# Paired FFN products on 64 rows beside the attention scores

## The chip, the core and the metric

The kernel runs on one core of a Trainium2 chip. The core has a matrix engine (TensorE, PE in the profile, with its weight loads as PEld), a vector engine (VectorE, DVE), a scalar engine (ScalarE, ACT), GpSimd (POOL) and SyncE (SP); each works through its own queue in order, and the queues wait for each other by semaphores. In this kernel POOL and SP mostly issue DMAs. The metric is the device time of one execution in microseconds (us), lower is better. Before the change it is 320.61 us, the median of 6 runs (319.83 to 321.36).

## What is computed

Attention with a bias by distance for 8 batches of 8 heads, 576 positions and 64 elements a head; the heads' outputs side by side are the input of a feed-forward network (FFN) with a maximum of three products:

```python
scores = q @ k.T / sqrt(64) + bias            # per batch and head, 576 x 576
attn = exp(scores - max) / sum(exp(...))
x = (attn @ v)                                # -> 4608 tokens x 512
h = maximum(maximum(x @ w1, x @ w2), x @ w3)  # 512 -> 768
out = h @ w_out                               # 768 -> 512
```

## The kernel before

**Attention by head pairs.** Two heads of 64 elements share the 128 partitions: head `par` of a pair lies on rows 64*par to 64*par+63 of the transposed queries and keys `qT` and `kT`. The main loop (line 813) goes over batches 1 to 7 and the four head pairs of each; (b, hp) names one, from 0. The 576 positions are four tiles of 128 and a left-over of 64.

- `visit` (line 554) makes the scores of 256 queries, c = 0 or 1, against the four key tiles: two groups of four matmuls, each on 64 rows, the two heads at once in two banks, and one exponential over each group into the tile `e4`. With `el` given it makes the scores of the 64 left queries (`scq`) first, in two banks of `ps_a`.
- `left_keys` makes the scores of the 64 left keys of both heads (`sct`) in one product on 128 rows.
- The bias enters as a product of exponentials: `times_band`, `times_bandt` and `times_band_left` multiply a band of `e4` or `el` on VectorE.
- `attend` (line 604; its matmuls are on line 94 in the profile, tile `a`) multiplies the exponentials by the values for half of the queries: 18 matmuls in half 0, 27 in half 1. The `quotients` that it returns divide on VectorE (a reciprocal, then a multiplication into `x_sb`). A head pair's two halves run in the next head pair, from the list `late`: half 0 after the first visit, half 1 in the hook `keys`.

**FFN between them.** A batch's tokens are turned by DMA transposes into `xT`. `ffn` makes, for a chunk of 512 tokens, six blocks of 128 hidden columns: `first` (a product of four matmuls over 128 rows each and 512 columns; copied by ScalarE into `m0`), `second` (product; VectorE's maximum with `m0` gives `m`) and `third` (product; maximum with `m` gives a block of `hT`), and then four `output` products of six matmuls each, copied to `osb` and stored through SP. These pieces wait in the list `pending` with their number of matmuls; `fill(target)` (line 439) takes pieces up to that number and puts hooks between them. In most head pairs there are two fills of up to 13, one before and one after the second visit, so a head pair holds 24 FFN matmuls.

**What holds the order.** Instructions passed to `inorder` keep the program's order on their engine; all matmuls do. PSUM (the matmuls' output memory) has eight banks: `ps_s` has two tiles of two banks for scores, `ps_a` two of one bank for `attend` (and `scq`, and some products), `ps_f` two of one bank for FFN products. A tile's next user waits until the last reader of the one before is done. `go_behind` makes given instructions wait for another one. `idle_sums` marks fills in which `first` may take a `ps_a` bank. On SP's queue stand, in program order, the stores of outputs (`store_outputs`), the DMA transposes of the next batch's q and k (`crossbar`, ten a batch, two at a time) and those of `x_sb`.

Of the kernel before, what the change touches and what calls it, by code (L numbers as in the profile page):

```python
# [10 lines left out]
F32 = mybir.dt.float32  # L11
# [28 lines left out]
def kernel(  # L40
# [52 lines left out]
    def mm(*args, **kw):  # L93
        inorder(nc.tensor.matmul(*args, **kw))  # L94
# [11 lines left out]
    def act_copy(out_, in_):  # L106
        return inorder(nc.scalar.activation(out=out_, in_=in_, func=ACTF.Copy))  # L107
# [206 lines left out]

    def ffn(t0, nt, last):
        hT = ffnw.tile([P, FCH * CH], BF16, tag="hT", name="hT")
        per = CH // nt
        n_fb = FCH // per  # L320
        st = [{} for _ in range(n_fb)]

        def product(ps, fb, ki):
            for i in range(per):
                cf = fb * per + i
                for c in range(DCH):
                    mm(
                        ps[:, i * nt : i * nt + nt], lhsT=w_bf[ki][:, c, cf * P : cf * P + P],
                        rhs=xT[:, c, t0 : t0 + nt], start=(c == 0), stop=(c == DCH - 1),
                    )  # L330

        def bank(name):
            return ps_f.tile([P, CH], F32, tag="ff", name=name)

        def block(fb):
            return hT[:, fb * CH : fb * CH + CH]

        def first(fb):
            ps0 = ps_a.tile([P, CH], F32, tag="a", name="ps0") if last or idle_sums else bank("ps0")
            product(ps0, fb, 0)  # L340
            if per > 1:
                nc.scalar.activation(out=block(fb), in_=ps0, func=ACTF.Copy)
                return
            st[fb]["m0"] = ffnw.tile([P, CH], BF16, tag="m0", name="m0")
            nc.scalar.activation(out=st[fb]["m0"][:], in_=ps0, func=ACTF.Copy)  # L345

        def second(fb):
            ps1 = ps_s.tile([P, 2 * CH], F32, tag="sc", name="ps1")[:, 0:CH] if last else bank("ps1")
            product(ps1, fb, 1)
            if per > 1:  # L350
                inorder(nc.vector.tensor_tensor(out=block(fb), in0=ps1, in1=block(fb), op=ALU.max))
                return
            m = st[fb]["m"] = ffnw.tile([P, CH], BF16, tag="m", name="m")
            inorder(nc.vector.tensor_tensor(out=m[:], in0=ps1, in1=st[fb]["m0"][:], op=ALU.max))  # L354

        def third(fb):
            ps2 = bank("ps2")
            product(ps2, fb, 2)
            other = block(fb) if per > 1 else st[fb]["m"][:]
            inorder(nc.vector.tensor_tensor(out=block(fb), in0=ps2, in1=other, op=ALU.max))  # L360

        def output(j):
            osb = osbp.tile([P, d_model], F32, tag="osb", name="osb")
            r0 = t0 + j * P

            def columns(ps, c0, c1):
                for cf in range(FCH):
                    mm(
                        ps, lhsT=hT[:, cf * nt + j * P : cf * nt + j * P + P], rhs=wo_bf[:, cf, c0:c1],
                        start=(cf == 0), stop=(cf == FCH - 1),  # L370
                    )

            if r0 + P == NTOK:
                c = d_model - P
                for copy, c0, c1, pool, tag, eng in (
                    (dve_copy, 0, c, ps_f, "ff", nc.sync), (act_copy, c, d_model, ps_a, "a", nc.scalar)
                ):
# [12 lines left out]
            if last:  # L390
                store()
            else:
                stores.append(store)

        f, m, g = ([(DCH, lambda fn=fn, fb=fb: fn(fb)) for fb in range(n_fb)] for fn in (first, second, third))
        o = [(FCH, lambda j=j: output(j)) for j in range(nt // P)]
        if per == 1:
            portions = [[f[0], m[0]]]
            for fb in range(1, n_fb):
                portions.append([g[fb - 1], f[fb], m[fb]])  # L400
            portions.append([g[-1], (0, None), o[0]])
        else:
            if not t0:
                portions = [[f[0]], [m[0], f[1]], [m[1]], [f[2], m[2]]]
                deferred.append(([[g[0]], g[1:]], [[x] for x in o]))
                o = []
            else:
                portions = [x for gs, _ in deferred for x in gs]
                for fb in range(n_fb):
                    portions += [[f[fb], m[fb]], [g[fb]]]  # L410
                portions += [x for _, os in deferred for x in os] + [[o[0]]]
                o = o[1:]
        if len(o) > 2:
            portions.append(o[1:3])
        return portions, o[-1:]

    pending, rest, stores, deferred, idle_sums = [], [], [], [], []

    def store_outputs():

# [115 lines left out]
            ))  # L536

    def exp(out_, in_):
        nc.scalar.activation(out=out_, in_=in_, func=ACTF.Exp, scale=inv_sqrt_d)  # L539

    def put_left_queries(el, banks):

# [4 lines left out]
    def turn_left_queries(qT, kT, banks):  # L547

        for t in range(KT):
            for par, bank in enumerate(banks):  # L550
                r = slice(64 * par, 64 * par + 64)
                mm(bank[:, 64 * t : 64 * t + 64], lhsT=kT[r, P * t : P * t + P], rhs=qT[r, QM:S])

    def visit(qT, kT, e4, c, mid=None, el=None):

        if el is not None:
            banks = [ps_a.tile([P, KT * 64], F32, tag="a", name="scq") for _ in range(2)]
            turn_left_queries(qT, kT, banks)
            put_left_queries(el, banks)
        for tt in range(0, KT, 2):  # L560
            sc = ps_s.tile([P, 2, 2, QS], F32, tag="sc", name="sc")
            for t in range(2):
                for par in range(2):
                    r = slice(64 * par, 64 * par + 64)
                    mm(
                        sc[:, par, t, :], lhsT=kT[r, P * (tt + t) : P * (tt + t) + P],
                        rhs=qT[r, c * QS : c * QS + QS],
                    )
            exp(e4[:, tt : tt + 2, :, c * QS : c * QS + QS].rearrange("p t h q -> p h t q"), sc[:])
            if tt == 0 and mid:  # L570
                mid()

# [9 lines left out]


    def times_bandt(hp, el):
        inorder(nc.vector.tensor_tensor(
            out=el[:, S - 192 : S], in0=el[:, S - 192 : S], in1=bandt[:, hp, :], op=ALU.mult
        ))

    def left_queries(hp, qT, kT, el):

        sc = ps_s.tile([P, 2, CH], F32, tag="sc", name="scq")
        turn_left_queries(qT, kT, [sc[:, par, 0 : KT * 64] for par in range(2)])
        eq = el[:, S:].rearrange("p (t h q) -> p h t q", t=KT, h=2)
        exp(eq, sc[:, :, 0 : KT * 64].rearrange("p h (t q) -> p h t q", t=KT))

    def times_band_left(hp, el):
        last_tile = el[:, S + P * KT - P :].rearrange("p (h q) -> p h q", h=2)
# [160 lines left out]
    for hp in range(HP):  # L758
# [7 lines left out]
        def keys():  # L766
            left_keys(hp, qT, kT, el, QS, S)
# [45 lines left out]
    for b, hp in [(b, hp) for b in range(1, B) for hp in range(HP)]:  # L813
# [2 lines left out]
        qT, kT = (x[:, hp, :] for x in qk[b])  # L816
        e4, el = e_tiles()
        together = b > 1 and (b, hp) != (2, 0)
        rate = 8 if b == 1 or (b, hp) == (2, 0) else 13


# [12 lines left out]
        if turned:  # L834
            turned.pop(0)()
        quotients = next_late()
        times_band(hp, e4, 0, 0, QS, inorder)
        quotients()
        if b == 1 and hp + 1 < HP:
            spread_packed(hp + 1, nc.vector)  # L840
# [5 lines left out]
            if together:  # L846
                next_late()()

        fill(rate, keys, *([lambda: None] if together else []))
        times_bandt(hp, el)  # L850


        visit(qT, kT, e4, 1, el=el if together else None)
        store_outputs()
        if b == 1 or hp in (1, 2) and b + 1 < B:
            next(crossbar, None)
# [7 lines left out]
        if b == 1 and hp + 1 < HP:  # L864
            second_transposes(qk[1], hp + 1)
        if hp == 1 and b > 1:
            add_ffn((b - 1) * CH, CH)
        if hp == (2, 2, 0)[min(b, 3) - 1] and b + 1 < B:
            if b == 1:
                load_last_weights(turned_qk[2, 1, 1])  # L870
# [14 lines left out]
            for t in range(1 if together else 2, 3):  # L885
                times_band(hp, e4, t, 0, QM, inorder)

        if together:
            idle_sums.append(hp)
        fill(rate, bands_2, queries)  # L890
        idle_sums.clear()
        times_band_left(hp, el)
        for half in range(2):
            late.append(lambda b=b, hp=hp, e4=e4, el=el, half=half: attend(b, hp, e4, el, half))

    while late:
        store_outputs()
        early()
        next_late()()
        fill(13)  # L900
# [38 lines left out]
```

The softmax here doesn't subtract the row's maximum and nothing guards it: scores larger than these inputs give would overflow.

## Time and profile before

| | |
|---|---|
| median of 6 runs | 320.61 us |
| the profiled execution | 320.67 us, of which span 318.9 us |
| granted TensorE clock | 1.0 |
| PE busy | 308.1 us, 97% |
| DVE, ACT, POOL busy | 67%, 63%, 34% |
| all products of xT and w_bf, 512 columns | 576, one 379 ns |
| exponentials of 1024 columns | 128, one 1027 ns |

An instruction's duration is from its start to its end; matmuls are pipelined, so that the next one starts long before the end of the one before. Where PE works without pause, the distance between starts is what a matmul costs. The page also divides the span into 40 slices; PE's busy tenths, the granted clock and the DMA share show that the middle of the kernel is one even stage:

```profile
PE   7978899999999999999999999999999999999995
...
PEclk9999999999999999999999999999999999999999
DMA  9999999999999999999999999984032103301103
```

Each digit is a share in tenths of one slice of 8 us. From about 82 us (batch 3 of 8, third head pair) to 258 us (end of the last head pair) head pairs with FFN pieces follow each other; after it the FFN of the last chunks runs alone.

### The profile page before, as it was taken

The page shows a single profiled execution, that of the slowest core. Times are in us where ns is not written, and L with a number is a line of the kernel's source. Part 1 is how long each engine was busy: PE and PEld are TensorE (multiplying, and loading weights), DVE is VectorE, ACT ScalarE, POOL GpSimd, SP SyncE. Part 2 cuts the span into 40 slices and gives each one's busy share as a digit, 9 for nine tenths or more (in the row PEclk, how much of TensorE's full clock was granted, in tenths as well). Part 3 has the DMA queues.
Part 4 walks back from the last instruction along what each step waited for, and adds up shares of the span by engine and source line. Part 5 has one row for each costly group of instructions (what it writes and reads, how often), then busy time and mean ns, then how long its engine had stood idle before and what let it go on. Part 6 is the DMA issues. An engine that isn't in the chain of part 4 may idle for free.

```text
span 318.9 us, 8238 instructions
## 1 busy us (share of the span) xinstructions
PE 308.1 (97%) x3328; PEld 172.0 (54%) x3328; DVE 213.1 (67%) x535; ACT 201.4 (63%) x297; POOL 108.1 (34%) x143
## 2 busy tenths in 40 slices
PE   7978899999999999999999999999999999999995
PEld 2446777775555555555555555555555554444442
DVE  6386778786667766666667767777767675554552
ACT  3888898896777667766777677767776741122221
POOL 8938831358049711950294058300000000000000
PEclk9999999999999999999999999999999999999999
DMA  9999999999999999999999999984032103301103
GB/s 166 199 197 199 182 152 138 125 109 141 201 147 153 146 203 139 122 122 197 161 135 139 216 124 133 140 188 96 5 74 99 36 2 74 134 0 72 61 0 132
DMA packets 163878, 40.34 MB, mean 126 GB/s; under 512 B 153720, under 2 KB 159360, under 8 KB 163840
## 3 DMA queue, kind: packets, MB, share of 16 engines
q0 software_dynamic: 103776, 16.66, 76.8%
q1 hardware_dynamic: 58304, 22.69, 38.1%
q10 hardware_dynamic: 1760, 0.47, 0.7%
q8 instruction: 26, 0.43, 0.5%
q14 instruction: 12, 0.10, 0.1%
HBM read 35.39 MB, written 9.45 MB: 141 GB/s over the span
## 4 chain that ended last, share of the span: by engine, by line
PE 74%; DMA 1%; ACT 1%; issue 0%
PE ps L94 40%; PE pso L94 13%; PE a L94 11%; PE sc L94 7%; PE sct L94 2%; PE scq L94 2%; DMA out_dram<-osb 1%; ACT e L539 0%; ACT osb L388 0%; ACT osb L107 0%
## 5 line engine op out<-in xcount | busy, mean ns | idle before, releaser
L94 PE MATMUL ps<-xT,w_bf 128*128 128x512 bf16 (+1 forms) x720 | 152.2, 358 | 0.6 <-ACT xT L107 0.6
L539 ACT ACTIVATE e<-sc 128x1024 bf16<-128x1024 f32 x128 | 124.4, 1027 | 19.5 <-PE sc L94 17.0
L94 PEld LDWEIGHTS <-w_bf 128*128 128x128 bf16 x720 | 65.4, 98 | 63.4 <-issue 5.8
L533 DVE TENSOR_TENSOR e<-e,hank 128x512 bf16<-128x512 bf16 (+2 forms) x136 | 58.6, 467 | 9.7 <-ACT e L539 9.4
L345 ACT ACTIVATE m<-ps 128x512 bf16<-128x512 f32 x48 | 29.2, 608 | 51.9 <-PE ps L94 51.9
L354 DVE TENSOR_TENSOR m<-ps,m 128x512 bf16<-128x512 f32 x48 | 33.1, 689 | 34.1 <-PE ps L94 34.0
L94 PEld LDWEIGHTS <-kT 64*128 64x128 bf16 (+1 forms) x832 | 30.4, 95 | 38.6 <-issue 25.2
L94 PE MATMUL pso<-wo_bf,hT 128*128 128x512 bf16 (+2 forms) x222 | 50.3, 373 | 0.0
L94 PE MATMUL a<-vx,e 128*128 128x65 bf16 x1024 | 44.9, 193 | 0.0
L94 PE MATMUL sc<-qT,kT 64*128 64x256 bf16 x512 | 41.9, 278 | 2.1 <-ACT e L539 0.9
L360 DVE TENSOR_TENSOR hT<-ps,m 128x512 bf16<-128x512 f32 x48 | 33.1, 689 | 15.9 <-PE ps L94 14.4
L94 PEld LDWEIGHTS <-e 128*128 128x128 bf16 x1024 | 40.7, 97 | 0.8
L167 POOL DMA_DIRECT2D q_sb<-in_q_dram x24 | 22.0, 918 | 47.1 <-DMA kT<-k_sb 16.0
L139 POOL DMA_DIRECT2D vx<-in_v_dram x32 | 28.4, 910 | 25.4 <-DMA kT<-k_sb 13.6
L94 PE MATMUL a<-vt,el 128*128 128x130 bf16 x160 | 35.5, 222 | 0.0
L110 DVE COPY osb<-pso 128x512 f32<-128x512 f32 (+1 forms) x33 | 22.6, 686 | 17.9 <-PE pso L94 14.7
L641 DVE TENSOR_TENSOR x_sb<-a,rd 128x256 bf16<-128x256 f32 (+1 forms) x64 | 31.4, 491 | 2.2
L539 ACT ACTIVATE el<-scq 128x256 bf16<-128x256 f32 (+1 forms) x55 | 20.6, 417 | 19.3 <-PE scq L94 19.2
L94 PEld LDWEIGHTS <-hT 128*128 128x128 bf16 x222 | 20.1, 98 | 22.4 <-issue 1.5
L94 PEld LDWEIGHTS <-el 128*128 128x128 bf16 x416 | 24.1, 97 | 9.3 <-issue 5.7
L539 ACT ACTIVATE el<-sct 128x576 bf16<-128x576 f32 (+2 forms) x36 | 21.6, 603 | 5.4 <-PE sct L94 4.0
L167 POOL DMA_DIRECT2D k_sb<-in_k_dram x24 | 22.1, 921 | 1.3 <-DMA w_bf<-in_moe_w_dram 1.2
(71 smaller groups left out, 172.1 us busy)
## 6 DMA issues: line engine op xcount, KB each, us to landing
out_dram<-osb SPq DMA_DIRECT2D x35, 256.0 KB, 2.4
vx<-in_v_dram POOLq DMA_DIRECT2D x32, 128.0 KB, 7.0
q_sb<-in_q_dram POOLq DMA_DIRECT2D x26, 128.0 KB, 5.2
k_sb<-in_k_dram POOLq DMA_DIRECT2D x24, 128.0 KB, 5.8
w_bf<-in_moe_w_dram POOLq DMA_DIRECT2D x3, 768.0 KB, 10.1
xT<-in_k_dram SPq DMA_DIRECT2D x6, 128.0 KB, 4.5
hank<-w_dr SPq DMA_DIRECT2D x2, 384.0 KB, 6.3
wo_bf<-in_moe_w_out_dram POOLq DMA_DIRECT2D x1, 768.0 KB, 8.0
```

The source lines that it names most:

```text
L94: inorder(nc.tensor.matmul(*args, **kw))
L110: return inorder(nc.vector.tensor_copy(out_, in_))
L139: in_turn(b, nc.gpsimd.dma_start(out=dst[:, t, h0:h1, :], in_=x[:, t, h0:h1, :])) for t in range(t0, t1)
L167: loads.append(in_turn(b, nc.gpsimd.dma_start(out=dst[:, t], in_=main_part(src, b)[:, t])))
L345: nc.scalar.activation(out=st[fb]["m0"][:], in_=ps0, func=ACTF.Copy)
L354: inorder(nc.vector.tensor_tensor(out=m[:], in0=ps1, in1=st[fb]["m0"][:], op=ALU.max))
L360: inorder(nc.vector.tensor_tensor(out=block(fb), in0=ps2, in1=other, op=ALU.max))
L533: put(nc.vector.tensor_tensor(out=e4[:, t, :, lo:hi], in0=e4[:, t, :, lo:hi], in1=hank[:, 2 * hp : 2 * hp + 2, c0:c1][:, :, ::-1], op=ALU. ...
L539: nc.scalar.activation(out=out_, in_=in_, func=ACTF.Exp, scale=inv_sqrt_d)
L641: divided[b, hp, half] = inorder(nc.vector.tensor_tensor(out=x_sb[b][:, 2 * half : 2 * half + n, P * hp : P * hp + P].rearrange("p t (h d) ...
```

## The change

From head pair (2, 2) on, the 22 head pairs that follow are *tiled*. `ffn` returns *stages* instead of pieces. A stage has two pairs of products. A pair computes two products in two banks, each matmul of 128 rows split into two of 64: in a first pass (`rows(False)`) product 0 runs on the lower rows and product 1 on the upper ones, in a second pass (`rows(True)`, with `swap`) the other way round. A gates stage pairs `first` and `second` of one block in `ps_a` and those of the next block in `ps_f`, and leaves the two `third` products as pieces for the next head pair. The outputs stage pairs the four outputs. A chunk's four stages fall on (b, 2), (b, 3), (b+1, 0) and (b+1, 1); the chunk that starts at (7, 1) has two of them, and the rest of it as pieces after the loop.

```diff
+        def pair(n, operands, pool, tag):
...
+            def rows(swap, behind=()):
+                if not swap:
+                    ps.extend(pool.tile([P, CH], F32, tag=tag, name="psp") for _ in range(2))
...
+                for c in range(n):
+                    for par in range(2):
+                        i = par ^ swap
+                        lhsT, rhs = operands[i](slice(64 * par, 64 * par + 64), c)
+                        made.append(inorder(nc.tensor.matmul(
+                            ps[i][:], lhsT=lhsT, rhs=rhs, start=not swap and c == 0, stop=swap and c == n - 1,
+                        )))
+                for ins in behind:
+                    go_behind(made[:1], ins)
...
+            def two(fb, pool, tag):
+                ps, rows = pair(DCH, (gate(fb, 0), gate(fb, 1)), pool, tag)
+                def end(behind):
+                    rows(True, behind)
+                    m0 = ffnw.tile([P, CH], BF16, tag="m0", name="m0")
+                    act_copy(m0[:], ps[0][:])
+                    def larger():
+                        m = st[fb]["m"] = ffnw.tile([P, CH], BF16, tag="m", name="m")
+                        inorder(nc.vector.tensor_tensor(out=m[:], in0=ps[1][:], in1=m0[:], op=ALU.max))
+                    return larger
+                return lambda: rows(False), end
+            return two(fb, ps_a, "a") + two(fb + 1, ps_f, "ff") + ([g[fb], g[fb + 1]],)
...
+            return two(0, ps_a, "a", (act_copy, dve_copy)) + two(2, ps_f, "ff", (dve_copy, dve_copy)) + ([],)
```

In a tiled head pair the second visit is taken apart, and the 64-row passes stand between its scores. The next head pair's first visit follows directly, also on 64 rows. The left queries go back to a `ps_s` tile with one exponential. Two waits are added: the first matmul of `end0` waits for the left queries' exponential, that of `end1` for `times_bandt`, which itself waits for the last matmul of `begin1`.

```diff
-        fill(rate, keys, *([lambda: None] if together else []))
-        times_bandt(hp, el)
-        visit(qT, kT, e4, 1, el=el if together else None)
+        if tiled:
+            fill(FCH)
+            keys()
+            fill(FCH)
+            times_band(hp, e4, 0, 0, QS, inorder)
+            begin0, end0, begin1, end1, after = stages.pop(0)
+            scores(qT, kT, e4, 1, 0)
+            begin0()
+            exp_left = left_queries(hp, qT, kT, el)
+            turned_1 = begin1()
+            times_band(hp, e4, 1, 0, QM, inorder)
+            band_left = times_bandt(hp, el)
+            go_behind([band_left], turned_1[-1])
+            times_band_left(hp, el)
+            scores(qT, kT, e4, 1, 2)
+            dve0 = end0([exp_left])
+            dve1 = end1([band_left])
+            times_band(hp, e4, 2, 0, QM, inorder)
+            dve0()
+            dve1()
+            times_band(hp, e4, 3, 0, QM, inorder)
+            pending.extend((n, [fn]) for n, fn in after)
+        else:
+            fill(8 if (b, hp) == (2, 1) else rate, keys, *([lambda: None] if together else []))
+            times_bandt(hp, el)
+            visit(qT, kT, e4, 1, el=el if together else None)
         store_outputs()
...
         if hp == 1 and b > 1:
-            add_ffn((b - 1) * CH, CH)
+            pending.extend((n, [fn]) for n, fn in rest)
+            rest.clear()
+            made, tail = ffn((b - 1) * CH, CH, False, True)
...
-        fill(rate, bands_2, queries)
-        times_band_left(hp, el)
+        if not tiled:
+            fill(rate, bands_2, queries)
+            times_band_left(hp, el)
+        if hp == 1 and b > 1:
+            stages.extend(made)
+            strict.append(b)
...
+    pending.clear()
+    rest.extend(tail.pop())
+    pending.extend((sum(n for n, _ in p), [fn for _, fn in p]) for p in tail)
+    strict.clear()
+    fill(DCH)
```

`scores` is one group of `visit`'s body with its exponential. While `strict` is set, the exponentials keep the program's order on ScalarE. `idle_sums` goes: before the last chunks `first` takes a `ps_f` bank. The first fill of (2, 1) takes 8 instead of 13.

More of the change, by code (lines that the diff above doesn't have):

```diff
@@ L312, in make_bandt, with ffn @@
             dve_copy(bandt[r, :, :], hank[r, par::2, c : c + 192][:, :, ::-1])
-    def ffn(t0, nt, last):
+    def ffn(t0, nt, last, tiled=False):
         hT = ffnw.tile([P, FCH * CH], BF16, tag="hT", name="hT")
@@ L338, in first @@
         def first(fb):
-            ps0 = ps_a.tile([P, CH], F32, tag="a", name="ps0") if last or idle_sums else bank("ps0")
+            ps0 = ps_a.tile([P, CH], F32, tag="a", name="ps0") if last else bank("ps0")
             product(ps0, fb, 0)
@@ L393, in output @@
                 stores.append(store)
+        def pair(n, operands, pool, tag):
+            ps = []
+            def rows(swap, behind=()):
+                if not swap:
+                    ps.extend(pool.tile([P, CH], F32, tag=tag, name="psp") for _ in range(2))
+                made = []
+                for c in range(n):
[7 more added lines that the diff above has]
+                    go_behind(made[:1], ins)
+                return made
+            return ps, rows
@@ new lines, in gates, with gate @@
+        def gates(fb):
+            def gate(fb, ki):
+                return lambda r, c: (w_bf[ki][r, c, fb * P : fb * P + P], xT[r, c, t0 : t0 + nt])
+            def two(fb, pool, tag):
[10 more added lines that the diff above has]
+            return two(fb, ps_a, "a") + two(fb + 1, ps_f, "ff") + ([g[fb], g[fb + 1]],)
@@ new lines, in outputs, with columns, two, end @@
+        def outputs():
+            def columns(j):
+                return lambda r, cf: (hT[r, cf * nt + j * P : cf * nt + j * P + P], wo_bf[r, cf, :])
+            def two(j, pool, tag, copies):
+                ps, rows = pair(FCH, (columns(j), columns(j + 1)), pool, tag)
+                def end(behind):
+                    rows(True, behind)
+                    def put(i):
+                        osb = osbp.tile([P, d_model], F32, tag="osb", name="osb")
+                        copies[i](osb[:], ps[i][:])
+                        r0 = t0 + (j + i) * P
+                        stores.append(lambda: inorder(nc.sync.dma_start(out=out[r0 : r0 + P, :], in_=osb[:])))
+                    if copies[0] is act_copy:
+                        put(0)
+                        return lambda: put(1)
+                    return lambda: (put(0), put(1))
+                return lambda: rows(False), end
+            return two(0, ps_a, "a", (act_copy, dve_copy)) + two(2, ps_f, "ff", (dve_copy, dve_copy)) + ([],)
@@ L395, in ffn @@
         f, m, g = ([(DCH, lambda fn=fn, fb=fb: fn(fb)) for fb in range(n_fb)] for fn in (first, second, third))
         o = [(FCH, lambda j=j: output(j)) for j in range(nt // P)]
+        if tiled:
+            tail = [g[2:4]] + [[x[fb] for x in (f, m, g)] for fb in (4, 5)]
+            return [gates(2 * i) for i in range(n_fb // 2)] + [outputs()], tail + [[x] for x in o]
         if per == 1:
@@ L415, in ffn @@
         return portions, o[-1:]
-    pending, rest, stores, deferred, idle_sums = [], [], [], [], []
+    pending, rest, stores, deferred, stages, strict = [], [], [], [], [], []
     def store_outputs():
@@ L538, in exp @@
     def exp(out_, in_):
-        nc.scalar.activation(out=out_, in_=in_, func=ACTF.Exp, scale=inv_sqrt_d)
+        made = nc.scalar.activation(out=out_, in_=in_, func=ACTF.Exp, scale=inv_sqrt_d)
+        return inorder(made) if strict else made
     def put_left_queries(el, banks):
@@ L552, in turn_left_queries, with scores @@
                 mm(bank[:, 64 * t : 64 * t + 64], lhsT=kT[r, P * t : P * t + P], rhs=qT[r, QM:S])
+    def scores(qT, kT, e4, c, tt):
+        sc = ps_s.tile([P, 2, 2, QS], F32, tag="sc", name="sc")
+        for t in range(2):
+            for par in range(2):
+                r = slice(64 * par, 64 * par + 64)
+                mm(
+                    sc[:, par, t, :], lhsT=kT[r, P * (tt + t) : P * (tt + t) + P],
+                    rhs=qT[r, c * QS : c * QS + QS],
+                )
+        exp(e4[:, tt : tt + 2, :, c * QS : c * QS + QS].rearrange("p t h q -> p h t q"), sc[:])
     def visit(qT, kT, e4, c, mid=None, el=None):
@@ L560, in visit @@
         for tt in range(0, KT, 2):
[L561 to L569, printed above, removed]
+            scores(qT, kT, e4, c, tt)
             if tt == 0 and mid:
@@ L584, in times_bandt @@
     def times_bandt(hp, el):
-        inorder(nc.vector.tensor_tensor(
+        return inorder(nc.vector.tensor_tensor(
             out=el[:, S - 192 : S], in0=el[:, S - 192 : S], in1=bandt[:, hp, :], op=ALU.mult
@@ L593, in left_queries @@
         eq = el[:, S:].rearrange("p (t h q) -> p h t q", t=KT, h=2)
-        exp(eq, sc[:, :, 0 : KT * 64].rearrange("p h (t q) -> p h t q", t=KT))
+        return exp(eq, sc[:, :, 0 : KT * 64].rearrange("p h (t q) -> p h t q", t=KT))
     def times_band_left(hp, el):
@@ L818 @@
         together = b > 1 and (b, hp) != (2, 0)
+        tiled = bool(stages)
         rate = 8 if b == 1 or (b, hp) == (2, 0) else 13
@@ L836 @@
         quotients = next_late()
-        times_band(hp, e4, 0, 0, QS, inorder)
+        if not tiled:
+            times_band(hp, e4, 0, 0, QS, inorder)
         quotients()
@@ L847, in keys @@
                 next_late()()
-        fill(rate, keys, *([lambda: None] if together else []))
-        times_bandt(hp, el)
-        visit(qT, kT, e4, 1, el=el if together else None)
+        if tiled:
+            fill(FCH)
+            keys()
+            fill(FCH)
+            times_band(hp, e4, 0, 0, QS, inorder)
+            begin0, end0, begin1, end1, after = stages.pop(0)
[19 more added lines that the diff above has]
+            visit(qT, kT, e4, 1, el=el if together else None)
         store_outputs()
@@ L886, in bands_2 @@
                 times_band(hp, e4, t, 0, QM, inorder)
-        if together:
-            idle_sums.append(hp)
-        fill(rate, bands_2, queries)
-        idle_sums.clear()
-        times_band_left(hp, el)
+        if not tiled:
+            fill(rate, bands_2, queries)
[3 more added lines that the diff above has]
+            strict.append(b)
         for half in range(2):
             late.append(lambda b=b, hp=hp, e4=e4, el=el, half=half: attend(b, hp, e4, el, half))
+    pending.clear()
[3 more added lines that the diff above has]
+    fill(DCH)
     while late:
```

## The prediction

> **What bounds the kernel now.** I read the page first, then the timeline of one head pair of the stage that changes, then single starts in the trace. Times are microseconds (us).
>
> ```profile
> PE 308.1 (97%) x3328; PEld 172.0 (54%) x3328; DVE 213.1 (67%) x535; ACT 201.4 (63%) x297; POOL 108.1 (34%) x143
> ...
> L539 ACT ACTIVATE e<-sc 128x1024 bf16<-128x1024 f32 x128 | 124.4, 1027 | 19.5 <-PE sc L94 17.0
> ```
>
> TensorE (PE) is busy 97% of the span and no other engine passes 67%, and ScalarE (ACT) waits for the scores, not they for it. So time is gained only by making PE's sequence shorter, and lost by any pause in it. The timeline of one head pair, (5,3) with batch and pair counted from 0 as in the code, shows that sequence (start, duration, engine, line, what; x is the number of instructions):
>
> ```profile
> 185.69 0.61 PE L94 MATMUL sc<-qT,kT 64*128 64x256 bf16 x8
> ...
> 186.12 1.94 ACT L539 ACTIVATE e<-sc 128x1024 bf16<-128x1024 f32 x2 [0.48 <-PE sc L94]
> ...
> 186.23 0.23 PE L94 MATMUL a<-vt,el 128*128 128x130 bf16 x1
> ...
> 186.84 1.02 PE L94 MATMUL ps<-xT,w_bf 128*128 128x512 bf16 x4
> ...
> 187.71 0.41 PE L94 MATMUL sct<-qT,kT 128*128 128x512 bf16 x2
> ...
> 187.95 0.22 PE L94 MATMUL a<-vt,el 128*128 128x130 bf16 x1
> ...
> 188.85 1.89 PE L94 MATMUL ps<-xT,w_bf 128*128 128x512 bf16 x8
> 189.05 0.20 DVE L640 RECIPROCAL rd<-a 128x6 f32<-128x6 f32 x1 [0.29 <-PE a L94]
> 189.28 0.56 DVE L641 TENSOR_TENSOR x_sb<-a,rd 128x384 bf16<-128x384 f32 x1
> ...
> 190.67 0.29 PE L94 MATMUL scq<-qT,kT 64*128 64x64 bf16 x8
> ```
>
> No PE row has a bracket: PE waits for nobody. "64*128" is work on 64 rows, "128*128" on all. A head pair holds two blocks of 64-row work (185.69 and 190.67), so the array changes its mode four times in its 8.34 us (185.69 to the next 194.03).
>
> **What a change of mode costs.** 512-column products start 216 ns apart. The last before a 64-row block starts 311 ns ahead of it: 95 more. The first pair of scores takes 120 ns instead of 109: 11 more. On leaving, 205 instead of 109 (96), and the next step 68 instead of 57 (11). A block costs 95+11+96+11 = 0.213 us, and every block from 82 to 258 us repeats it within 5 ns. [...]
>
> **What the change removes.** 22 head pairs run in the new form, (2,2) to (7,3), counted from 0 as in the code. Each joins its second block to the next head pair's first; the last has no successor: 21 blocks less, 21 x 0.213 = **-4.5 us**.
>
> **What it adds to PE by itself.** A 128-row product becomes two of 64 rows in two banks, run together. 22 stages are used: five chunks of 512 tokens with three gates stages of 16 pairs and one outputs stage of 24, and two gates stages of the sixth chunk: 5 x 72 + 32 = 392 pairs, in place of as many products. In the trace 256-column score pairs start 109 ns apart, half of 216 and one, with both weight loads inside; so I take 216 ns for a 512-column pair and no cost; a gain I exclude, since today's products already start at the pace of their columns. [...] That two row tiles *accumulate* at full pace (scores don't) no row shows; at worst a pair costs two products, 392 x 0.216 = +85 us. Both operands stream as for the scores, so I hold it unlikely.
>
> **Where PE will wait.** The work per head pair is no longer even. Before it is 24 products each. Now gates stages hold 16 and leave two third products (8) to the next head pair; the outputs stage, (b,1), holds 24 and leaves nothing. So (b,2) has no product in either fill. I lay out such a head pair from its first score, t = 0:
>
> - Scores to 0.54. The first exponential starts 0.31 after its last score (185.81 to 186.12), at 0.43, and takes 1.02: 1.46.
> - Attend half 0, 18 matmuls, to 1.15. Then the left keys' scores (sct) want the bank of that exponential. PE starts 51 ns after an exponential that it waited for, as here, in an early stage:
>
> ```profile
> 18.37 1.96 ACT L539 ACTIVATE e<-sc 128x1024 bf16<-128x1024 f32 x2
> ...
> 19.46 0.30 PE L94 MATMUL sct<-qT,kT 128*128 128x320 bf16 x1 [0.80 <-ACT e L539]
> ```
>
>  So sct starts at 1.51: **0.36 lost**.
> - sct 0.24, attend half 1 0.90: 2.65. Change of mode and half of the scores: 2.98. Then the first pair wants both ps_a banks, and the second is held by half 1 until its quotients are done. Reciprocal 0.23 after the last matmul (2.62) at 2.85, multiplication at 3.08, 0.56 long, release 55 ns: 3.70. **0.72 lost.** In the lines above 8 products (1.8 us) lie between this quotient and the next use of ps_a.
> - After that nothing waits: 1.08 per (b,2), five times from b = 3: **+5.4 us**. The ends: 0 if both releases came early enough, and little over 1.1, since the rows that make up the two waits vary by 10 ns.
>
> The other head pairs have covers, with four products before and after sct: sct at 2.02 against 1.80 (the exponential is 0.3 later there, behind the m0 copy); begin0 at 4.35 (half 1 ends at 3.16, a fill of 0.86, 0.33 as above) against quotients at 4.21 (half 1's last matmul at 3.13, then 1.08 as above), a margin of only 0.14; end0 waits for the left queries' exponential, 6.18 against 6.43; end1 for the bandt product, itself held until begin1's last matmul ends (6.4), done 6.7 against 7.3. Behind that DVE wait stand two bands, both maxima and the next quotients; they finish 1.9 after the next head pair's start, before attend half 1 (2.3) reads the last band. Half 0 reads query columns below 256, which the late band of t = 3 doesn't write. If one of these covers failed by 0.1 us it would cost 1.7 us over 17 head pairs.
>
> **Edges.** At (2,1) the first fill is 8 instead of 13, so sct comes right after half 0 and waits 0.40; but 12 products instead of 6 stand before (2,2)'s scores, where PE now pauses (block of 1.13 us at 76.33 against 0.54): together -0.2. (2,2) still has six output products for sct, not for begin0: +0.7. After (7,3) the fill starts with a third product in the ps_f bank that the last m0 copy frees at 0.87; with 0.1 of mode change hidden in it: +0.67. Sum **+1.2**.
>
> **DMAs.** The four output stores now come together in SP's queue, at the end of (b,1), and wait for VectorE's copies about 1.5 us into (b,2). Behind them stand the transposes of the next batch's q and k, eight in a row at some 1.3 us. Counted from (b,1)'s start, their end moves from about 20.9 to 22.4, their use from 25.0 to 25.4. In the tightest batch of before the last landing that the scores read (125.56) was 1.8 us ahead of them (127.35), and the k tail (126.26) 3.1 ahead of sct. That leaves slack: I count 0 and keep 1 us for it. Moving exp into fixed order, the left queries to ps_s and the first product's bank at (2,1) move no PE work: 0.
>
> **Sum.** -4.5 + 5.4 + 1.2 = +2.1 us on the profiled execution (318.9 span, 320.67 with what lies around it; the median is 320.61): **322.8 us**.
>
> **Rivals.** Differences under 0.2% can't be told from none here: 319.97 to 321.25.
> 1. The forecast, 322.8, 0.62; its own range is 321 to 324.6.
> 2. Only the mode changes count: (b,2) doesn't wait, because exponentials and quotients come in time. Then -4.5 + 1.2 - 0.7 = -4.0: 316.7. For it: PE never waits today, and the total ACT and DVE load in (b,2) fits. Against it: only two banks in ps_a, and 0.33 us between half 1 and begin0 where the quotient rows need 1.05. It decides if a (b,2) loses under (4.5-1.2)/5 = 0.66. 0.15.
> 3. The stores hold the transposes back: some transposes took 2.1 to 2.9 us in SP's queue while loads ran. Eight at 2.2 are 7 us later, past the slack, and (b+1,0) waits 1 to 2.5 us in four batches: 327 to 333. Against it: the loads that crowded them are over sooner. 0.13.
> 4. [...] 0.10.
>
> Slower takes 0.55 of the first, all of the third, 0.08 of the fourth: 0.76. Same: 0.05 + 0.03 + 0.02 = 0.10. Faster: 0.02 + 0.12 = 0.14. The range 318.4 to 326.2 leaves out the body of rival 2 and the tails of 3 and 4.
>
> **What would show it.** In the profile after: 23 blocks of 64-row work from (2,2) on instead of 44; 216 ns between starts of pairs; in every (b,2) a bracket of about 0.4 on sct after an exponential and of 0.7 on the first paired product after x_sb; (b,1) near 9.9 us, (b,2) 7.5, the others 8.1. It is wrong if (b,2) shows no brackets, if other head pairs show some, or if scores of (b,0) wait for qT or kT.

## The result, and the profile after

| | median | runs | range |
|---|---|---|---|
| before, beside it | 320.67 us | 41 | 319.34 to 325.09 |
| after | 324.94 us | 20 | 321.32 to 395.94 |

After to before is 1.0092 [1.0066, 1.0118] (a 95% interval): slower, and the whole interval lies beyond the 0.2% that can't be told from no change. The ratio leaves out runs more than 1.5% above the fastest of their kernel, such as the one of 395.94 us at a mean granted clock of 0.76, so that after is 3.0 us (2.1 to 3.8) slower by it, and not the 4.3 between the two medians. The forecast was 322.8, or +2.1, its range 318.4 to 326.2.

The profile of after belongs to the execution of 395.94 us; so the one shown here is of e1_again, the same kernel run again (below). That execution took 327.25 us, span 325.5, and is the longest of its six. From its page, busy time, the granted clock in 40 slices of 8 us, and two groups (mean ns, then idle time of the engine before them):

```profile
PE 307.6 (95%) x3696; PEld 185.2 (57%) x3720; DVE 213.0 (65%) x530; ACT 203.3 (62%) x280; POOL 108.1 (33%) x143
...
PEclk9979999999999799999999999999999999999999
...
L610 ACT ACTIVATE e<-sc 128x1024 bf16<-128x1024 f32 x128 | 126.6, 1025 | 50.5 <-PE sc L94 47.4
...
L408 PE MATMUL psp<-xT,w_bf 64*128 64x512 bf16 x544 | 68.9, 376 | 2.1 <-DVE x_sb L716 2.1
```

PE's share fell from 97% to 95% in a longer span: PE now waits. The paired products (tile `psp`) wait for `x_sb`, the quotients, 2.1 us in all. The clock row has two dips that before's had not.

The even stage in a view by stretches, one batch from (b,1)'s second visit to the next (length, then PE's busy time and instructions, the other engines', granted clock, DMA share, GB/s; the share adds up packets that overlap, and so exceeds 1). After:

```profile
109.98:143.56 33.58, 32.88 (x450) 20.16 (x454) 23.45 (x55) 23.95 (x31) 18.47 (x23) 1.00 1.75 157
143.56:177.13 33.58, 32.88 (x450) 20.16 (x454) 23.47 (x56) 23.95 (x31) 12.00 (x15) 1.00 1.33 133
```

Before, one batch:

```profile
127.35:160.69 33.34, 33.34 (x382) 18.15 (x382) 23.59 (x58) 23.59 (x34) 16.42 (x22) 1.00 1.73 147
```

By this view PE's work per batch became 0.46 us less, and its waits 0.70: 33.34 to 33.58. The modelled ends of matmuls hide some of both. By starts it is four blocks less (-0.85) and 1.09 of waits in (b,2), which gives the same 33.58. One (b,1) and the (b,2) behind it, in the timeline of after:

```profile
146.71 2.75 PE L408 MATMUL psp<-wo_bf,hT 64*128 64x512 bf16 x24
149.30 0.60 PE L94 MATMUL sc<-qT,kT 64*128 64x256 bf16 x8
149.83 0.23 PE L94 MATMUL a<-vt,el 128*128 128x130 bf16 x1
...
150.80 0.41 PE L94 MATMUL sct<-qT,kT 128*128 128x512 bf16 x2 [0.19 <-ACT e L610]
...
152.26 0.38 PE L408 MATMUL psp<-xT,w_bf 64*128 64x512 bf16 x1
152.99 0.39 PE L408 MATMUL psp<-xT,w_bf 64*128 64x512 bf16 x2 [0.35 <-DVE x_sb L716]
```

A bracket counts from the modelled end of the matmul before, so it is shorter than the loss; starts give the loss. The 18 matmuls of attend half 0 take 0.61 where nothing waits, and `sct` starts 0.97 after their first (149.83): 0.36 lost. The two matmuls of a pair start 3 to 4 ns apart where nothing waits, yet here the second, in the bank that the quotients free, starts 0.73 after the first (152.26, 152.99). Both are in every (b,2), at the forecast's sizes.

The third wait was not in the forecast. It comes once, in (3,1):

```profile
104.78 0.23 PE L94 MATMUL a<-vt,el 128*128 128x130 bf16 x1 [2.36 <-DMA vt<-in_v_dram]
...
105.39 1.43 PE L94 MATMUL ps<-xT,w_bf 128*128 128x512 bf16 x3
106.61 0.69 PE L94 MATMUL sct<-qT,kT 128*128 128x512 bf16 x2
107.11 0.30 PE L94 MATMUL a<-vt,el 128*128 128x130 bf16 x1
```

Attend half 0 waits for the tails of batch 3's values (`vt`, those of the 64 left positions; batches are counted from 0). Behind the wait the durations are longer (0.30 for 0.22) although nothing changed in the work: from 105.90 to 109.31 the granted clock is 0.50. Block to block the wait costs 2.43 and the half clock 1.62, together 4.05.

### The profile page after: what moved, and what is told of

Same layout as the page of the kernel before. It is cut to its first block, busy times and chain, and to the rows that moved or that the text cites. A ratio compares the mean times of both kernels' runs of the same rounds, so it can differ in the third digit from the quotient of the medians.

```text
span 394.2 us, 8965 instructions
## 1 busy us (share of the span) xinstructions
PE 383.0 (97%) x3720; PEld 210.5 (53%) x3720; DVE 217.6 (55%) x530; ACT 208.0 (53%) x280; POOL 108.2 (27%) x143
## 4 chain that ended last, share of the span: by engine, by line
PE 93%; ACT 3%; DVE 1%; issue 1%
PE psp L408 28%; PE ps L94 27%; PE a L94 15%; PE sc L94 9%; PE pso L94 7%; ACT e L610 3%; PE sct L94 3%; PE scq L94 2%; PE tp L97 1%; PE warm L94 1%; DVE x_sb L716 1%; PE xp L97 0%; ACT el L610 0%; DVE rd L715 0%; PE spread L94 0%
## 5 line engine op out<-in xcount | busy, mean ns | idle before, releaser
L94 PE MATMUL ps<-xT,w_bf 128*128 128x512 bf16 (+1 forms) x448 | 115.8, 412 | 1.3 <-ACT m L107 0.7
L408 PE MATMUL psp<-xT,w_bf 64*128 64x512 bf16 x544 | 88.8, 461 | 1.5 <-DVE x_sb L716 1.5
L94 PEld LDWEIGHTS <-w_bf 128*128 128x128 bf16 x448 | 44.9, 108 | 46.8 <-issue 43.1
L408 PEld LDWEIGHTS <-w_bf 64*128 64x128 bf16 x544 | 35.1, 109 | 29.7 <-issue 20.1
L408 PE MATMUL psp<-wo_bf,hT 64*128 64x512 bf16 x240 | 36.6, 457 | 0.0
L139 POOL DMA_DIRECT2D vx<-in_v_dram x32 | 28.3, 916 | 20.6 <-DMA kT<-k_sb 12.7
L345 ACT ACTIVATE m<-ps 128x512 bf16<-128x512 f32 x14 | 8.4, 597 | 46.4 <-PE ps L94 46.4
L432 DVE TENSOR_TENSOR m<-psp,m 128x512 bf16<-128x512 f32 x34 | 23.5, 691 | 10.1 <-ACT m L107 9.8
L94 PE MATMUL pso<-wo_bf,hT 128*128 128x512 bf16 (+2 forms) x102 | 28.2, 448 | 0.0
L610 ACT ACTIVATE el<-scq 128x512 bf16<-128x512 f32 (+1 forms) x33 | 19.2, 585 | 15.2 <-PE scq L94 15.1
L107 ACT ACTIVATE m<-psp 128x512 bf16<-128x512 f32 x34 | 20.3, 597 | 11.1 <-PE psp L408 8.8
```

What stands on the lines that cost most here:

```text
L139: in_turn(b, nc.gpsimd.dma_start(out=dst[:, t, h0:h1, :], in_=x[:, t, h0:h1, :])) for t in range(t0, t1)
L408: made.append(inorder(nc.tensor.matmul(ps[i][:], lhsT=lhsT, rhs=rhs, start=not swap and c == 0, stop=swap and c == n - 1,)))
L432: inorder(nc.vector.tensor_tensor(out=m[:], in0=ps[1][:], in1=m0[:], op=ALU.max))
L610: made = nc.scalar.activation(out=out_, in_=in_, func=ACTF.Exp, scale=inv_sqrt_d)
```

## The experiments

Two mechanisms can lie behind the loss: **order** (the forecast: what is saved in mode changes is lost to waits in (b,2) and at the end) and **data** (loads and transposes that come too late for the new order).

**Again.** The kernel after, unchanged.

> The changed kernel once more, for a profile at the full granted clock. Theory (the sum of the prediction): pairs start 216 ns apart, 23 blocks of 64-row work from (2,2) on, (b,1) about 9.9 us, (b,2) 7.5 with pauses of 0.36 before sct and 0.72 before the first paired product, the others 8.1; 1.004 to 1.010 of before. Rival (clock): products on two row tiles at once lower the granted clock; then the clock is under 1.0 in the stage of the pairs, all head pairs are longer than 8.2 us, and runs differ by more than those of before.

Measured: 325.34 us (324.34 to 327.25, 6 runs), ratio 1.0137 [1.0099, 1.0175]. The profile is the one above. Its span less the 4.05 of (3,1) is 321.45. Besides, it reaches the scores at 66.91 that before's profile has at 66.48, ahead of any change: 0.43. (The clock's dip to 0.50 at 20.6 to 24.0, absent in before's profile, is the likely cause; this is not shown.) 321.45 - 0.43 = 321.02, against a forecast of 318.9 + 2.1 = 321.0 for the span. So in this execution the order costs what the forecast said, and the data came on top. The rival falls: the clock is 1.00 in both batches above, and in the execution of 395.94 us it was at 0.75 or less from 13 us on, long before the first pair.

**Outputs evened out.** The outputs stage keeps one pair; the other two outputs go as whole products into the fills of (b,2).

```diff
-            return two(0, ps_a, "a", (act_copy, dve_copy)) + two(2, ps_f, "ff", (dve_copy, dve_copy)) + ([],)
+            return two(0, ps_a, "a", (act_copy, dve_copy)) + (None, None, o[2:])
...
-            turned_1 = begin1()
-            times_band(hp, e4, 1, 0, QM, inorder)
+            if begin1:
+                turned_1 = begin1()
+                times_band(hp, e4, 1, 0, QM, inorder)
...
-            dve0 = end0([exp_left])
-            dve1 = end1([band_left])
+            dve0 = end0([exp_left] if begin1 else [band_left])
+            dve1 = end1([band_left]) if begin1 else lambda: None
```

> The outputs stage keeps one pair; the other two outputs go as whole products into the two empty fills of (b,2). Theory: (b,2) no longer waits, (b,1) waits at most 0.2 for the bandt product, so 5 x (1.08 - 0.16) = 4.6 us less than the changed kernel, about 0.995 of before. Rival (the loss is not in (b,2) but in the pairs or the clock): within 1.5 us of the changed kernel, whose pairs it keeps but for 60 of 392.

Measured: 322.47 (13 runs), ratio 1.0046 [1.0016, 1.0076], 2.9 us under e1_again beside it, where 4.6 were expected. Its profile, too, has a wait for values with half clock behind it (0.50), 2.39 us in (2,1), ahead of the changed stage. A batch of this kernel by stretches, and its (b,1) in the timeline:

```profile
141.33:174.41 33.08, 32.50 (x437) 18.76 (x441) 23.60 (x56) 23.80 (x31) 15.83 (x20) 1.00 1.72 154
```

```profile
142.97 0.38 PE L94 MATMUL sc<-qT,kT 64*128 64x256 bf16 x4
143.44 1.47 PE L408 MATMUL psp<-wo_bf,hT 64*128 64x512 bf16 x12
...
145.63 0.22 PE L94 MATMUL a<-vt,el 128*128 128x130 bf16 x1 [0.28 <-ACT osb L107]
```

The waits of (b,2) are gone from b = 3 on, a batch is 0.50 shorter. The expectation was 0.92 a batch, and missed two new waits that the rows show: the second pass starts 0.47 after the scores instead of 0.22, because it is held behind the bandt product, and half 0 waits for the copy of an output that has its bank.

**Other bank first.** In (b,2) alone the pair in `ps_f` goes first, that in `ps_a`, whose bank the quotients hold, second.

```diff
-            begin0()
+            (begin1 if hp == 2 else begin0)()
...
-            turned_1 = begin1()
+            turned_1 = (begin0 if hp == 2 else begin1)()
```

The two guards of `end0` and `end1` change places with them.

> In (b,2) alone the first passes change places: the pair in ps_f begins before the left queries, the one in ps_a after them, 0.86 us later. Theory: the 0.72 before begin0 goes; end0 now waits about 0.28 for the bandt product, which follows the later pass; the 0.36 before sct stays: 6 x 0.44 = 2.6 us less than the changed kernel. Rival (that wait costs nothing, because what follows it would wait anyway): no change.

Measured: 323.84 (10 runs), ratio 1.0083 [1.0057, 1.0109], 1.5 under e1_again where 2.6 were expected, with intervals that overlap. The trace is sharper: the block of 64-row work in (b,2) takes 4.86 us, after's 5.28, six times alike: 0.42 less for the 0.44 expected. (In (3,1) this profile has e1_again's wait for the values once more, 1.95 us, with the full clock, 1.00, behind it.) In the timeline of this kernel:

```profile
149.35 0.39 PE L94 MATMUL sc<-qT,kT 64*128 64x256 bf16 x4
149.58 1.03 PE L408 MATMUL psp<-xT,w_bf 64*128 64x512 bf16 x8
...
151.42 0.38 PE L94 MATMUL sc<-qT,kT 64*128 64x256 bf16 x4
151.94 1.90 PE L408 MATMUL psp<-xT,w_bf 64*128 64x512 bf16 x16
```

The first pair runs without a gap (0.23 behind the scores), so the 0.73 was the bank's; what is left, 0.30 at 151.94, is a second pass held by the bandt product.

**Whole products at the same places.** Each matmul of 64 rows and its partner become one of 128 rows. The order and the added waits stay, and the array changes its mode around every pass.

```diff
-                    for par in range(2):
-                        i = par ^ swap
-                        lhsT, rhs = operands[i](slice(64 * par, 64 * par + 64), c)
-                        made.append(inorder(nc.tensor.matmul(
-                            ps[i][:], lhsT=lhsT, rhs=rhs, start=not swap and c == 0, stop=swap and c == n - 1,
-                        )))
+                    lhsT, rhs = operands[swap](slice(0, P), c)
+                    made.append(inorder(nc.tensor.matmul(
+                        ps[swap][:], lhsT=lhsT, rhs=rhs, start=c == 0, stop=c == n - 1,
+                    )))
```

> The paired products at the same places, but whole: product 0 on 128 rows in the first pass, product 1 in the second. Same columns, four 64-row blocks a head pair instead of one. Theory: 3 x 22 more blocks at 0.213 = 14 us more than the changed kernel, little less where a pause hides some: 336 to 339. [...] Rival (clock): the granted clock is back at 1.0, and the time grows by clearly less than 12.

Measured: 331.84 (4 runs), ratio 1.0367 [1.0307, 1.0427]. A batch of this kernel:

```profile
141.64:177.03 35.39, 34.77 (x375) 17.59 (x382) 23.48 (x56) 24.25 (x31) 14.96 (x19) 1.00 1.60 149
```

A head pair of the even kind takes 8.755 us, after's 8.12: three blocks more, 0.635, or 0.212 each. That is the forecast's price of a block, found again by adding blocks instead of removing them. The total is 6.5 us over e1_again's, far less than the 14 expected, for a reason that I overlooked: a first pass of whole products needs only the first bank, so the wait of 0.73 in each (b,2) and most of that at the end don't occur here, about 5 us in all. So a batch is 1.81 longer than after's, twelve blocks at 0.212 less one 0.73. Besides, this profile has no wait for data; e1_again's has one, of 4.05 with the half clock. The granted clock is 1.00 in this batch, as it is in after's two batches, so that a lower clock for 64-row work isn't part of after's time.

**Batch 3's values earlier, in after.** In the profile of e1_again, the loads of the values (on POOL's queue) start behind the key transpose t = 3. They start 1.5 us later than before, 1.1 if the 0.43 is taken off: that transpose is issued 0.4 later, behind an output store in SP's queue, and takes 0.7 longer to land (4.46 for 3.74). After, then before:

```profile
93.64 3.53 POOL L139 DMA_DIRECT2D vx<-in_v_dram  x4 [14.74 <-DMA kT<-k_sb]
97.12 1.30 POOL L158 DMA_DIRECT2D vt<-in_v_dram  x2
```

```profile
92.11 3.53 POOL L139 DMA_DIRECT2D vx<-in_v_dram  x4 [13.63 <-DMA kT<-k_sb]
95.59 1.30 POOL L158 DMA_DIRECT2D vt<-in_v_dram  x2
```

Before, the two tail loads landed 4.0 and 3.6 us after their issue; after, 7.0 and 7.0. The likely reason, not tried by itself, is the transposes of `x_sb`: before, they run from 97.75 on, 1.5 us behind the second tail load (96.21); after, from 97.39 on, ahead of it (97.74). In e6_v_before below they run from 97.78 on, ahead of both tail loads (98.77, 99.39), which take 6.4 and 6.5. The edit:

```diff
-            load_v(b + 1, 0, H, turned_qk[b + 1, 1, KT - 1] if b < 3 else None)
+            load_v(b + 1, 0, H, turned_qk[b + 1, 1, KT - 1 - b // 2] if b < 3 else None)
```

> After, with one dependency changed: the four loads of batch 3's values go behind the second to last 128-column transpose of its keys (t = 2) instead of the last (t = 3). In the second profile of after, t = 2 landed at 90.1 us and t = 3 at 93.1, the loads of the values started at 93.6 and their tails landed at 104.1 and 104.7, and PE waited 2.36 us for them in (3,1), followed by 3.4 us at half clock: 4.05 us together. Theory (the late values are what lies between the forecast's steps and the measured time): the loads start about 3 us earlier, the tails land by 98 to 101 us, before their use at 102.4, the wait at 104.8 is gone, the span is 321 to 322 and the median 322.8 to 323.5, 2 us under after's. Rival (the DMA engines are crowded there whatever starts first): the tails stay late or another landing takes their place at (3,0), 324.5 to 326, like after.

Measured: 324.2 (323.14 to 324.73, 6 runs), ratio 1.0089 [1.0058, 1.012]: no gain over after (1.0092) that can be told, where 2 us were expected. The wait for `vt` is gone as expected, but in its timeline another has come up one head pair earlier:

```profile
97.03 0.42 PE L94 MATMUL sct<-qT,kT 128*128 128x512 bf16 x2 [1.16 <-DMA kT<-ktail]
```

The key tail's transpose, now issued beside the loads of the values, takes 5.8 us to land for 2.7 in e1_again. The span is 322.7, of which this block is 1.33 too long: 321.4 without it, again the order's own time (321.45). Theory and rival both held in part.

**Batch 3's values later, in before.** Nothing of PE's order is changed; the loads go behind the transpose of the key tail.

```diff
-        if hp == (2, 2, 0)[min(b, 3) - 1] and b + 1 < B:
+        if hp == (2, 3, 0)[min(b, 3) - 1] and b + 1 < B:
...
-            load_v(b + 1, 0, H, turned_qk[b + 1, 1, KT - 1] if b < 3 else None)
+            load_v(b + 1, 0, H, turned_qk[b + 1, 1, KT - 2 + b] if b < 3 else None)
```

(The next loads of q and k follow them in the same queue, and move with them.)

> The kernel before, with the loads of batch 3's values moved the other way: behind the transpose of the key tail (t = 4, landed 94.1 us in the profile of before) instead of t = 3 (91.6), and issued one head pair later, in (2,3). Nothing of the FFN's order is changed. Theory (it is the start of these loads, not the order of PE's work, that makes the stall in (3,1)): the tails of the values land about 2.5 us later or more, at 102 to 105 us against a use at 102.9, PE waits 0 to 2 us in (3,1), with up to 1.6 more where the clock falls behind it: 321.5 to 324.5, with a trace that shows the same wait for vt as after. Rival (the stall belongs to the changed order and needs it): within 0.5 us of before and no wait for vt.

Measured: 322.88 (22 runs), ratio 1.0075 [1.0052, 1.0099], with the wait in the timeline of (3,1):

```profile
105.91 0.22 PE L94 MATMUL a<-vt,el 128*128 128x130 bf16 x1 [1.96 <-DMA vt<-in_v_dram]
```

So the wait doesn't need the changed order; it needs values that start late. The clock stayed at 1.00 behind this one. (A second wait, 0.51 us for a key tail in (4,0), comes with the loads that moved along, so not all of the 1.0075 is the values'.)

**The best order.** From e2_even: the guard in (b,1) becomes a tiny VectorE instruction, an output product goes ahead of half 0 in (b,2), the other bank goes first in (2,2), and after the loop half 0 goes ahead of the first third product.

```diff
+        if hp == 2 < b:
+            fill(FCH)
...
+            else:
+                band_left = inorder(nc.vector.memset(mark[:], 0.0))
...
-    fill(DCH)
```

> The form with a pair and two whole products in the outputs stage (e2_even), with three more edits: the guard on the second pass of that stage is a tiny VectorE instruction instead of the whole bandt product; in (2,2) the pair in ps_f goes first (as in e3_order); in (b,2) a whole output product stands ahead of attend half 0, so that nothing waits for its copy; and after the loop attend half 0 goes ahead of the first third product, so that the wait of 0.75 us there is covered. By the rows of e2_even: its 0.25 and 0.28 us a batch go (5 x 0.53 = 2.6), 0.4 at (2,2), 0.6 after the loop: 3.6 us less than e2_even, which had 322.5: 318.5 to 319.5, a batch in 32.6 us, ratio to before 0.993. If the wait for the values in (3,1) doesn't occur in it, about 317.3, 0.99. Rival (other waits take their place, as m0's or the quotients'): no faster than e2_even, 321.5 to 323.

Measured: 321.03 (318.82 to 322.69, 14 runs), ratio 0.9989 [0.9959, 1.0019]: no difference from before, where 318.5 to 319.5 were expected. A batch takes 32.53 (below), 1.05 less than after's, as expected; but its timeline shows data waits of 4.86 us: in (2,1), ahead of the changed stage, and in (4,0).

```profile
142.69:175.22 32.53, 32.16 (x436) 18.70 (x442) 23.54 (x57) 23.80 (x31) 13.85 (x18) 1.00 1.73 143
```

```profile
73.67 0.22 PE L94 MATMUL a<-vt,el 128*128 128x130 bf16 x1 [3.40 <-DMA vt<-in_v_dram]
```

```profile
130.78 0.28 PE L94 MATMUL sc<-qT,kT 64*128 64x256 bf16 x2 [1.46 <-DMA kT<-k_sb]
```

**The best order with batch 3's values earlier**, twice, and **before with the same edit**. The edit is that of e5_v_after.

> e7_best with the loads of batch 3's values behind the transpose t = 2 as in e5_v_after. If the late values cost after about 2 us in its median, this one takes as much off e7_best: 317 to 317.8, ratio to before 0.988 to 0.991, faster than before. If they don't, it has e7_best's time within 0.5 us.

> The kernel before, with the edit of e5_v_after and e8_best_v alone: the loads of batch 3's values behind the key transpose t = 2 instead of t = 3. Theory (before reaches (3,1) with 3 us of slack, so an earlier start has nothing to win; it wins only in an order of PE's work that comes to the values sooner): within 0.7 us of before, and e8's gain over before is the order's, made visible by the earlier loads. Rival (the earlier loads are the gain themselves, in any order): 1.5 to 2.5 us faster than before, as e8 against e7.

> e8_best_v once more, beside e9_before_v on the same chip. If its gain holds: 317.5 to 319.5, ratio to before 0.989 to 0.996, and 1.5 to 3 us under e9_before_v. If it was the chance of seven runs: within 0.7 us of before.

Measured:

| | median | runs | ratio to before |
|---|---|---|---|
| e8_best_v | 318.87 | 7 | 0.9925 [0.988, 0.9971] |
| e10_best_v_again | 319.93 | 22 | 0.9951 [0.9924, 0.9978] |
| e9_before_v | 322.14 | 14 | 1.0017 [0.9987, 1.0046] |

The combination is faster than before by 0.5 to 0.75%, and so faster than after; both medians lie above their expectations, by 1.1 and 0.4 us. The earlier loads alone don't help before: its profile shows the wait for the key tail (1.57 us at 96.95). The same wait, larger, is in the profile of e10_best_v_again:

```profile
97.63 0.42 PE L94 MATMUL sct<-qT,kT 128*128 128x512 bf16 x2 [2.71 <-DMA kT<-ktail]
```

It isn't in that of e8_best_v, the same kernel, whose only wait for data is one of 0.90 in (5,0). So the stretch of batch 3's loads, where the DMA row stands at 9 tenths, has no slack left for either place; which load is late changes from one execution to the next. Less their waits for data, the spans of e7_best, e8_best_v and e10_best_v_again are 315.1, 315.4 and 314.9, against 318.9 before: this order is worth 3.5 to 4 us, of which late data took a part back in each of the three.

## Why the prediction was right, and where it was not

- **Changes of mode, -4.5.** Right. 23 blocks of 64-row work from (2,2) on instead of 44, and e4_apart gives 0.212 for a block against 0.213.
- **Pairs at 216 ns, no cost.** Right, and so rival 4 (0.10), dearer pairs, falls. (b,1)'s block of 24 pairs takes 6.276, an even head pair's with 16 pairs 4.549: 0.216 for each of the eight. The second matmul of a pair starts 3 to 4 ns behind the first, and the next pair 216 ns behind that pair's start. No run shows a surcharge on a pair; what the runs showed in its place is this 0.216, for products that accumulate on two row tiles.
- **The waits of (b,2), 0.36 + 0.72, +5.4.** Right: 0.36 and 0.73, in every batch. e3_order moves the second by its bank, e2_even removes both. Rival 2 falls with it. The periods came out at 9.85, 7.48 and 8.12 for 9.9, 7.5 and 8.1, and no other head pair waits, though one cover was put at only 0.14.
- **Edges, +1.2.** Right in what could be read: (2,2)'s block is 0.73 longer than an even one (0.7), and the last block, less the scores that no longer follow in it, 0.75 longer (0.67). (2,1) with (2,2)'s first scores is 0.2 shorter, as forecast.
- **DMAs, counted 0, kept 1.** This is the term that was too small. The order by itself gives +2.1 by the trace, as summed. The ratios give +3.0 (2.1 to 3.8) and in e1_again +4.4 (3.2 to 5.6), so 0.9 to 2.3 us lie on top. The profile has a wait on data of 2.43 in (3,1) with 1.62 of half clock behind it, but that is one execution, the longest of its six. e3_order's has the same wait, 1.95; e4_apart's and before's have none. I looked for the danger where the change moves DMAs, at the four stores and the transposes behind them from (b,1) on, and took the slack of batches 4 to 7. The place that broke was batch 3's values: a chain of landings (key transpose, then the loads, then their use) in the stretch where the DMA row stands at 9 tenths, with 3 us of slack in before's trace (landed at 99.85, used at 102.9). There the loads started 1.1 later and took 3 longer to land. Rival 3 named another chain and 1 to 2.5 us in four batches; in the two profiles of after no such wait is seen. Single ones appeared in e7_best's (4,0), 1.46, and e8_best_v's (5,0), 0.90.

That the number came within 1 us of the ratio's is the order's sum, not luck; that it stayed in the range with the data put at nothing is in part luck, since their share can be more than the 1 us kept for it.

That values which start later bring this wait is shown by e6_v_before. That they matter to a faster order is likely from e8_best_v and e10_best_v_again against e7_best (2.2 and 1.1 us by the medians, with intervals that overlap at their ends). What stays open is how the 0.9 to 2.3 us divide over the executions, of which only a few are traced: the earlier loads brought another wait in place of the first. Half clock is a small part at most: from the mean clocks on record I estimate 1.7 stretches of 3.41 us a run in e1_again and 1.4 in before beside it, so 0.3 x 1.6 = 0.5 us. Whether the four stores together have a share wasn't tried by itself.

## What to carry to other kernels

Price a change of the array's mode from the gaps at a boundary in your own trace, count the boundaries, and the saving can come out to a few hundredths of a us, as here; then look for the instructions whose cover the new order uses up, because the saving is only worth what is left after their waits. Evenness can be worth as much as the saving: here two of the four output products moved to the next head pair, with a shorter guard, took a batch from 33.58 to 32.53, where the saved changes of mode were worth 0.85. And check slack at the latest load of the busiest DMA stretch, not only at the DMAs that the change moves: here 3 us were not enough.

## What the hardware showed besides

Twice a wait of PE had half clock behind it: after waits of 2.36 (e1_again) and 2.39 us (e2_even) the granted clock was 0.50 for 3.41 us, in e1_again 1.62 us more. After waits of 1.95 (e3_order), 1.96 (e6_v_before), 2.71 (e10_best_v_again) and 3.40 us (e7_best) it stayed at 1.00. So the length of the wait alone didn't decide; what did is not shown.

Other stretches at 0.50 stand early in the traces: 20.55 to 23.96 in e1_again, 11.32 to 14.74 in e2_even, 20.03 to 23.44 in after, 3.41 us each, and 7.88 to 14.71 in e10_best_v_again, 6.83 us.
